# A Fourier-domain mixer and a gated feed-forward block on one core: the transform's operations put in order by a list scheduler in the source

## The chip, the cores and the metric

The kernel runs on one core of a Trainium2 chip. The metric is the time of one execution on the device in microseconds, lower is better: 2671.5 us as the median of three runs (2670.18 to 2675.18). The core's engines are TensorE (PE, with its weight loads shown apart as PEld), VectorE (DVE), ScalarE (ACT), GpSimd (POOL) and SyncE (SP), which issues all of the kernel's DMAs here. Every engine works through its own list of instructions in order; semaphores make one wait for another.

## The reference

```python
def _attn_ref(x, w_r, w_i, b_r, b_i):                 # x: 8 x 3008 x 256
    X = np.fft.rfft(x, axis=1)
    Xr, Xi = X.real, X.imag
    Yr = Xr @ w_r - Xi @ w_i + b_r
    Yi = Xr @ w_i + Xi @ w_r + b_i
    Yr = np.sign(Yr) * np.maximum(np.abs(Yr) - 0.01, 0.0)   # the same for Yi
    ...
    return np.fft.irfft(Yr + 1j * Yi, n=3008, axis=1)

def _moe_ref(x, w_gate, w_val, w_out):                # 24064 rows, 256 -> 1536 -> 256
    g = x @ w_gate
    return (g * (1.0 / (1.0 + np.exp(-g))) * (x @ w_val)) @ w_out
```

The second function is applied to the first one's output.

## The kernel before, in words

There are two phases. The transform (the function `transform`) does the Fourier part, the mixing by `w_r` and `w_i`, the soft threshold and the inverse transform, and it writes its result to DRAM as `xt_d`. The feed-forward block (`gated_ffn`) then runs 24 blocks of tokens through products on TensorE, whose order of instructions is fixed in the source (`tc.manual_schedule`). Both phases split their operands into a high part and a rest and make three products for one.

The transform cuts the 3008 samples into 47 x 64. Three kinds of work make it up:

- A **chunk** (16 for each of 8 batches): SP loads 96 x 512 numbers (`load_x`, L334), TensorE multiplies them by `wa` (`stage_a`, L357), and VectorE transposes the product into `d1` (L359). The 16 chunks of batch 0 run first, at the start; the 112 of the other seven run beside the pairs of the batch before.
- A **pair** of frequencies (12 for each batch, 96 in all) goes through stages. `stage_b` makes four products into the bank `ps_b` (L368; each is two recorded matmuls), ScalarE and VectorE split them into `f_hi`, `f_lo` and a sum `f` (L377 to L381). `stage_sum` makes six products of the sum (L391), and VectorE adds the bias and spreads the result over the bank `mixb` (L393). `stage_mix` makes twelve products onto it (L404); ScalarE gathers the result into `t` with four copies (L416), VectorE clips (L417), GpSimd subtracts (L418), ScalarE and VectorE split it into `y_hi` and `y_lo` (L421, L422). `stage_bi` makes three products (L435; six halves at L432 for the first pair of a batch), ScalarE copies them to `z` (L438) and SP stores `z` to the DRAM tile `d2` (L439).
- A **unit** (8 for each of 7 batches, 56 in all): SP loads `z_in` from `d2` (`load_z`, L445), TensorE makes eight products for two banks (`stage_ai`, L454; sixteen recorded matmuls), ScalarE copies them (L461) and SP stores to `xt_d` (L462). Batch 7's units are made inside the feed-forward block.

Beside this run 18 conversions of the feed-forward weights from 64-bit to 32-bit floats (`load_weights` and `load_seven`): SP loads `raw` (L263), VectorE does eight integer and float steps (L270 to L279), GpSimd five (L280 to L294), ScalarE a copy (L301), GpSimd the rest (L302), and SP stores. At the end the first block's inputs for the feed-forward are fetched and split (`feed.load`, `feed.sum`, `feed.part`, L148 to L166).

What sets the order: the source puts each stage of each pair, chunk, unit and conversion into a numbered slot (`at(slot, fn)`; pair j's four stages are in slots j to j+3, a conversion's `raw` load in one slot and its first three VectorE steps in the next), and `run(slot)` traces them slot by slot. From this trace the framework's own scheduler chooses the order on each engine by a simulated timeline. A few edges of order are given by hand: loads are issued behind the latest store of `z` (`paced`), a slot's stores behind the latest load (`run`), and a unit's products behind the `stage_bi` products of three pairs back (`second`).

Of the kernel before, what the change touches and what calls it, by code (L numbers as in the profile page):

```python
# [18 lines left out]
B = 8  # L19
# [23 lines left out]
LEAD, Z_LEAD = 1, 2  # L43
Z_FIRST = 18
Z_LATE, Z_AT, Z_STEP = 48, 90, 1
W_FIRST, W_STEP = 14, 3.8
FEED = 84
WARM = 1
# [72 lines left out]

class Feed:
# [34 lines left out]
    def part(self, blk, n_, eng):  # L157
# [8 lines left out]
        eng.tensor_tensor(part[:, 1, :h], src, f32(part[:, 0, :h]), op=ALU.subtract)  # L166
# [29 lines left out]
def transform(ctx, tc, front, ring, last, ps_, feed, xp, w_r, w_i, cb, wup_raw, wdn_raw, ca, cf, ci, co, w21, wup_d, wdn_d, xt_d, d2):  # L196
# [37 lines left out]
    def load_mix():  # L234
# [16 lines left out]
        for q in (1, 3):  # L251
            v.tensor_scalar_mul(bias[0][32 * q : 32 * q + 32, 0, :], bias[0][32 * q : 32 * q + 32, 0, :], -1.0)
# [7 lines left out]
    def load_weights(src):  # L260

        raw = ring.tile([P, 14 * P], I32, name="raw64", tag="wup")[:, : 2 * T].rearrange("p (a b) -> p a b", b=2)
        paced(lambda: nc.sync.dma_start(raw.rearrange("p a b -> p (a b)"), src))  # L263
        yield
        low, high = raw[:, :, 0], raw[:, :, 1]
# [4 lines left out]
        v.tensor_scalar(e, high, 20, 0x7FF, op0=ALU.logical_shift_right, op1=ALU.bitwise_and)  # L270
        v.tensor_scalar(e, e, 896.0, 1150.0, op0=ALU.max, op1=ALU.min)
        v.tensor_scalar(e, e, 896.0, float(1 << 23), op0=ALU.subtract, op1=ALU.mult)
        yield
        v.scalar_tensor_tensor(a.bitcast(I32), high, -(1 << 31), e, op0=ALU.bitwise_and, op1=ALU.bitwise_or)
        v.tensor_scalar(e, low, 8, None, op0=ALU.logical_shift_right)
        v.scalar_tensor_tensor(b, e, 2.0**-44, a, op0=ALU.mult, op1=ALU.mult)  # L276
        yield
        v.tensor_scalar(e, high, 0xFFFFF, 0x100000, op0=ALU.bitwise_and, op1=ALU.bitwise_or)
        v.scalar_tensor_tensor(a, e, 2.0**-20, a, op0=ALU.mult, op1=ALU.mult)  # L279
        nc.gpsimd.tensor_tensor(a, a, b, op=ALU.add)  # L280
        yield w, raw

    def load_seven(src, kind, u):

        for res in load_weights(src):
            if res is None:
                yield
        w, _ = res
        g = nc.gpsimd
        a21, a11, a12, a22, s1, s2, s3, s4 = [w[:, i, :] for i in range(8)]  # L290
        g.tensor_tensor(s1, a21, a22, op=ALU.add)
        g.tensor_tensor(s2, s1, a11, op=ALU.subtract)
        g.tensor_tensor(s3, a11, a21, op=ALU.subtract)
        g.tensor_tensor(s4, a12, s2, op=ALU.subtract)  # L294
        if kind == "down" and u == NQ - 1:
            nc.scalar.copy(w21[:, 0], a21)
            g.tensor_tensor(w21[:, 1], a21, f32(w21[:, 0]), op=ALU.subtract)
        w = w[:, 1:8, :]
        both = ring.tile([P, 2, 7, P], F32R, name="wup")
        hi, lo = both[:, 0], both[:, 1]  # L300
        nc.scalar.copy(hi, w)  # L301
        nc.gpsimd.tensor_tensor(lo, w, f32(hi), op=ALU.subtract)  # L302
        nc.sync.dma_start((wup_d if kind == "up" else wdn_d)[u], f32(both.rearrange("p i n a -> p i (n a)")))


    stores, loads, products, pending = [], [], [], []
    marks = {}

    def run(slot):
        held = pending[:]  # L310
        pending.clear()
        for fn in slots[slot]:
            fn()
        with tc.issue_after(loads[-1].ins) if loads else ExitStack():
            for fn in held:
                fn()

    def behind(p, fn):
        with ExitStack() as order:
            for mark in marks[B - 1, p]:  # L320
                order.enter_context(tc.issue_after(mark.ins))
            fn()

    def paced(fn):
        with tc.issue_after(stores[-1].ins) if stores else ExitStack():
            return fn()

    def second(fn):
        with tc.issue_after(products[-3].ins):
            fn()  # L330

    def load_x(b, ch):
        t = take()
        loads.append(nc.sync.dma_start(t, xp[b, ch]))  # L334
        return t
# [18 lines left out]
    def stage_a(b, ch, xt):  # L354
        tag = "absz"[ch % 4] if b == 0 else "a"
        ps = ps_.tile([P, T], F32, name="ps_a", tag="ps_" + tag)
        nc.tensor.matmul(ps, lhsT=wa, rhs=xt, start=True, stop=True)  # L357
        to = d1[b % 2][:, :, ch * CW : (ch + 1) * CW, :].rearrange("p k c i -> p c k i")
# [3 lines left out]
    def stage_b(b, p):  # L362
        t = d1[b % 2][:, p]
        ps = ps_.tile([P, T], F32, name="ps_b")
        for cc in range(2):
            for k in range(2):
                s = (cc * 2 + k) * P
                nc.tensor.matmul(ps[:, s : s + P], lhsT=t[:, cc * P : (cc + 1) * P, k], rhs=wf[:, 2 * p + k, :], start=True, stop=True)  # L368

        total = sb.tile([P, 2 * P], F32, name="f", tag="f", bufs=2)  # L370
        hi = sb.tile([P, 3, 2, P], F32R, name="f_hi", tag="f_hi", bufs=3)
        lo = sb.tile([P, 3, 2, P], F32R, name="f_lo", tag="f_lo", bufs=3)
        both = ps.rearrange("p (a q b) -> p a q b", q=2, b=64)
# [3 lines left out]
        nc.scalar.copy(first(hi), both)  # L377
        nc.scalar.copy(blocks(total), both[:, :, 0])
        v.tensor_tensor(blocks(total), blocks(total), both[:, :, 1], op=ALU.add)
        split = v.tensor_tensor(first(lo), both, f32(first(hi)), op=ALU.subtract)  # L380
        marks[b, p] = nc.scalar.copy(flat(hi), total), split, nc.gpsimd.tensor_tensor(flat(lo), total, f32(flat(hi)), op=ALU.subtract)  # L381
        return hi, lo

    def stage_sum(b, p, parts):

        mixb = mixed[p % 2]
        p1 = ps_.tile([P, T], F32, name="ps_s")
        n = 0
        for cc in range(2):
            for w, x in PASSES:  # L390
                nc.tensor.matmul(p1[:, :C], lhsT=parts[x][:, 2, cc, :], rhs=wmix[0][w][:, cc, :], start=n == 0, stop=n == 5)  # L391
                n += 1
        v.tensor_tensor(  # L393
            mixb.rearrange("p (a c) -> p a c", c=C), p1[:, :C].rearrange("p (a c) -> p a c", a=1).to_broadcast([P, 2, C]), bias[0], op=ALU.add
        )
        return parts

    def stage_mix(b, p, parts):

        mixb = mixed[p % 2]  # L400
        for half, (q, i) in enumerate(((1, 2), (0, 1))):
            for cc in range(2):
                for w, x in PASSES:
                    nc.tensor.matmul(  # L404
                        mixb[:, half * C : (half + 1) * C],
                        lhsT=parts[x][:, q, cc, :],
                        rhs=wmix[i][w][:, cc, :],
                        start=False,
                        stop=(cc, w) == (1, 1),
                        skip_group_check=True,  # L410
                    )
        t = sb.tile([P, T], F32, name="t", tag="t", bufs=2)
        y = sb.tile([P, T], F32, name="y", tag="y", bufs=2)
        for k in range(2):
            for half in range(2):
                nc.scalar.copy(t[64 * half : 64 * half + 64, k * C : (k + 1) * C], mixb[64 * k : 64 * k + 64, half * C : (half + 1) * C])  # L416
        v.tensor_scalar(y, t, LAM, -LAM, op0=ALU.min, op1=ALU.max)  # L417
        nc.gpsimd.tensor_tensor(t, t, y, op=ALU.subtract)  # L418
        hi = sb.tile([P, T], F32R, name="y_hi", tag="y_hi")
        lo = sb.tile([P, T], F32R, name="y_lo", tag="y_lo")  # L420
        nc.scalar.copy(hi, t)  # L421
        v.tensor_tensor(lo, t, f32(hi), op=ALU.subtract)  # L422
        return hi, lo

    def stage_bi(b, p, parts):
        if p == 0 and b < B - 1:
            d2[b] = dram.tile([NK, P, C], F32, name="d2", tag="d2")
        ps = ps_.tile([P, T], F32, name="ps_z")
        if p == 0:
            for k in range(2):  # L430
                for n, (w, x) in enumerate(PASSES):
# [453 lines left out]
```

## Time and profile before

| what | value |
|---|---|
| median of three runs | 2671.5 us |
| the profiled execution's own time | 2670.4 us |
| its span | 2668.6 us |
| PE busy, share of the span | 2637.2 us, 99% |
| DVE / ACT / POOL busy | 78% / 64% / 76% |
| mean granted clock of TensorE | 0.998 |

The span runs from the first to the last instruction. A matmul's recorded duration includes its way through the array, and the durations of neighbours overlap; the time that one costs in a full stream is the distance between two starts. The transform takes about the first 625 us. The granted clock is a fraction of 2.4 GHz; 0.50 is the level of 1.2 GHz.

### The profile page before, as it was taken

The page shows a single profiled execution, that of the slowest core. Times are in us where ns is not written, and L with a number is a line of the kernel's source. Part 1 is how long each engine was busy: PE and PEld are TensorE (multiplying, and loading weights), DVE is VectorE, ACT ScalarE, POOL GpSimd, SP SyncE. Part 2 cuts the span into 40 slices and gives each one's busy share as a digit, 9 for nine tenths or more (in the row PEclk, how much of TensorE's full clock was granted, in tenths as well). Part 3 has the DMA queues.
Part 4 walks back from the last instruction along what each step waited for, and adds up shares of the span by engine and source line. Part 5 has one row for each costly group of instructions (what it writes and reads, how often), then busy time and mean ns, then how long its engine had stood idle before and what let it go on. Part 6 is the DMA issues. An engine that isn't in the chain of part 4 may idle for free.

```text
span 2668.6 us, 39333 instructions
## 1 busy us (share of the span) xinstructions
PE 2637.2 (99%) x13170; PEld 2210.8 (83%) x13170; DVE 2079.5 (78%) x3035; ACT 1706.1 (64%) x3342; POOL 2035.7 (76%) x1574
## 2 busy tenths in 40 slices
PE   9999999999999999999999999999999999999999
PEld 6888878898888888888888888888888888888899
DVE  6878777756877787787877887778777887888787
ACT  4767667686665666666666666666666666666665
POOL 3546545556888888888888888888888888888886
PEclk9999999999999999999999999999999999999999
DMA  5576666676544444455445544454444444444453
GB/s 150 179 220 220 208 222 215 226 227 226 185 152 154 164 156 152 149 167 166 144 143 166 167 154 149 154 165 167 152 143 159 164 150 136 163 163 152 150 174 129
DMA packets 141402, 452.53 MB, mean 170 GB/s; under 512 B 13777, under 2 KB 61617, under 8 KB 141105
## 3 DMA queue, kind: packets, MB, share of 16 engines
q1 hardware_dynamic: 141200, 450.02, 51.4%
q8 instruction: 105, 1.72, 0.3%
q14 instruction: 97, 0.79, 0.1%
HBM read 359.01 MB, written 90.96 MB: 169 GB/s over the span
## 4 chain that ended last, share of the span: by engine, by line
PE 87%; DVE 5%; DMA 3%; ACT 1%; POOL 1%; issue 1%; SPq 0%; ACTq 0%; DVEq 0%; POOLq 0%
PE bank L558 75%; PE mixb L404 3%; PE ps_a L357 2%; DMA raw<-wup 2%; PE ps_b L368 2%; PE ps_x L454 2%; PE ps_s L391 1%; PE ps_z L435 1%; DMA raw<-wdn 1%; PE bank L793 1%; DVE y_lo L422 1%; POOL t L418 1%; DVE d L359 1%; DVE mixb L393 0%; DVE scratch L276 0%
## 5 line engine op out<-in xcount | busy, mean ns | idle before, releaser
L558 PE MATMUL bank<-x_near,wup 128*128 128x512 f32 (+1 forms) x4032 | 1038.4, 386 | 0.4 <-DVE bank L732 0.2
L578 POOL TENSOR_TENSOR h_parts<-more,h_parts 128x512 fp32r<-128x512 f32 (+1 forms) x572 | 847.5, 1495 | 110.4 <-ACT h_parts L574 96.7
L558 PEld LDWEIGHTS bank<-x_near,wup 128*128 128x128 f32 x4032 | 750.4, 188 | 152.0 <-DVE bank L732 3.6
L558 PE MATMUL bank<-h_parts,wdn 128*128 128x512 f32 (+1 forms) x3021 | 835.9, 385 | 0.3 <-DVE h_parts L578 0.3
L578 POOL TENSOR_TENSOR h_parts<-hidden,h_parts 128x512 fp32r<-128x512 f32 (+1 forms) x431 | 564.5, 1320 | 204.7 <-ACT h_parts L574 176.0
L558 PEld LDWEIGHTS bank<-h_parts,wdn 128*128 128x128 f32 x3021 | 564.6, 188 | 109.2 <-DVE h_parts L578 0.7
L574 ACT CAST h_parts<-hidden 128x512 fp32r<-128x512 f32 (+1 forms) x433 | 265.7, 614 | 450.3 <-DVE hidden L705 450.3
L558 PE MATMUL bank<-x_parts,wup 128*128 128x512 f32 (+1 forms) x2016 | 526.7, 384 | 0.0
L705 DVE TENSOR_TENSOR hidden<-hidden,bank 128x512 f32<-128x512 f32 (+1 forms) x576 | 376.1, 674 | 77.9 <-PE bank L558 69.5
L558 PEld LDWEIGHTS bank<-x_parts,wup 128*128 128x128 f32 x2016 | 375.2, 188 | 71.4 <-DVE bank L732 1.7
L599 DVE TENSOR_TENSOR sums<-sums,bank 128x512 f32<-128x512 f32 (+1 forms) x357 | 240.3, 673 | 243.7 <-PE bank L558 243.6
L574 ACT CAST h_parts<-more 128x512 fp32r<-128x512 f32 (+1 forms) x572 | 349.3, 611 | 39.2 <-DVE more L569 28.5
L703 ACT ACTIVATE hidden<-bank 128x512 f32<-128x512 f32 (+1 forms) x432 | 252.5, 585 | 114.4 <-PE bank L558 114.0
L569 DVE TENSOR_TENSOR more<-hidden 128x512 f32<-128x512 f32 (+1 forms) x286 | 291.8, 1059 | 0.0
L569 DVE TENSOR_TENSOR more<-hidden,more 128x512 f32<-128x512 f32 (+1 forms) x286 | 257.6, 901 | 0.0
L418 POOL TENSOR_TENSOR t<-t,y 128x512 f32<-128x512 f32 x96 | 127.3, 1326 | 147.7 <-DVE y L417 137.0
L710 ACT COPY bank<-bank 128x512 f32<-128x512 f32 (+1 forms) x288 | 161.6, 561 | 109.3 <-DVE hidden L705 103.9
L732 DVE TENSOR_TENSOR bank<-hidden,bank 128x512 f32<-128x512 f32 (+1 forms) x288 | 197.0, 684 | 36.3 <-PE bank L558 23.7
L718 ACT COPY hidden<-bank 128x512 f32<-128x512 f32 (+1 forms) x288 | 167.6, 582 | 2.5
L381 POOL TENSOR_TENSOR f_lo<-f,f_hi 128x256 fp32r<-128x256 f32 x96 | 82.7, 861 | 104.2 <-ACT f_hi L381 96.0
L416 ACT COPY t<-mixb 64x256 f32<-64x256 f32 x384 | 140.9, 367 | 32.0 <-PE mixb L404 27.7
L166 POOL TENSOR_TENSOR x_near<-xf,x_near 128x512 fp32r<-128x512 f32 (+1 forms) x112 | 142.6, 1290 | 5.1 <-PE bank L558 4.8
(102 smaller groups left out, 3332.8 us busy)
## 6 DMA issues: line engine op xcount, KB each, us to landing
wup<-wup_d SPq DMA_DIRECT2D x288, 896.0 KB, 4.6
out<-o SPq DMA_DIRECT2D x88, 256.0 KB, 6.1
scratch<-xp SPq DMA_DIRECT2D x116, 192.0 KB, 3.5
d<-z SPq DMA_DIRECT2D x84, 256.0 KB, 2.3
z_in<-d SPq DMA_DIRECT2D x56, 384.0 KB, 4.7
xt_d<-xt SPq DMA_DIRECT2D x56, 376.0 KB, 5.4
xf<-xt_d SPq DMA_DIRECT2D x15, 1024.0 KB, 7.4
wup_d<-wup SPq DMA_DIRECT2D x12, 896.0 KB, 5.2
```

The costliest lines, as they stand in the source:

```text
L166: eng.tensor_tensor(part[:, 1, :h], src, f32(part[:, 0, :h]), op=ALU.subtract)
L418: nc.gpsimd.tensor_tensor(t, t, y, op=ALU.subtract)
L558: nc.tensor.matmul(o, lhsT=weights[w], rhs=parts[x], start=start and i == 0, stop=stop and i == 2, skip_group_check=True)
L569: v.tensor_tensor(at(o, h), at(a, h), at(b, h), op=ALU.subtract)
L574: act.copy(pair[i][:, 0, :h], at(i, h))
L578: eng.tensor_tensor(pair[i][:, 1, :h], at(i, h), f32(pair[i][:, 0, :h]), op=ALU.subtract)
L599: v.tensor_tensor(o, o, spare[:, :h], op=ALU.add)
L703: act.activation(at(i, h), src, AF.Silu)
L705: v.tensor_tensor(at(i, h), at(i, h), src, op=ALU.mult)
L710: act.copy(b3[:, :h], b1[:, :h])
L718: act.copy(m5, b2[:, :h])
L732: v.tensor_tensor(b2[:, :h], m5, b3[:, :h], op=ALU.add)
```

## The change

The slots, `run`, `paced`, `second` and `behind` are gone. Each piece of the transform is given to a `Plan` as an operation with a name, an engine, a cost in microseconds, a key (its place in a nominal timetable of 6.0 us a pair), the operations that it needs (data, and buffers that must be free) and a function that traces it. `Plan.order()` then goes through simulated time: for each engine it takes, of the first 160 waiting operations by key, those whose needs are already placed, and of those that could start within a margin (`NEAR`) of the earliest, the one with the lowest key; a key gives precedence and holds nothing back. `wide` operations are those of VectorE for which the plan reckons with GpSimd running beside them. The result is traced under `tc.manual_schedule` on all five engines, SP among them, up to the last pair's `second`; what comes after is traced in the plan's order and left to the framework's scheduler. The operations themselves are the same, but for the negation of two strips of the bias, which goes from VectorE to ScalarE.

```diff
-LEAD, Z_LEAD = 1, 2
-Z_FIRST = 18
-Z_LATE, Z_AT, Z_STEP = 48, 90, 1
-W_FIRST, W_STEP = 14, 3.8
+Z_FIRST = 18.5
+Z_LATE, Z_AT, Z_STEP = 48, 90.5, 1
+W_FIRST, W_STEP = 12, 3.85
 FEED = 84
+REACH = 160
+LOOSE = 95
+SLOT = 6.0
...
+class Plan:
+    TAIL = {"PE": 0.165, "ACT": 0.113, "DVE": 0.085, "POOL": 0.045, "SP": 0.0}
+    LAG = {"PE": 0.055, "ACT": 0.035, "DVE": 0.035, "POOL": 0.1, "SP": 0.05}
+    NEAR = {"PE": 0.1, "ACT": 0.2, "DVE": 0.2, "POOL": 0.3, "SP": 0.1}
...
+    def order(self):
+        ops = self.ops
+        waiting = sorted(ops, key=lambda name: ops[name][3])
+        end, start, free = {}, {}, dict(self.free)
+        pool_until = wide_until = -1e9
+        line = []
+        while waiting:
+            best = {}
+            for name in waiting[:REACH]:
+                engine, cost, tail, key, needs, fn, wide = ops[name]
+                if any(n not in end for n in needs):
+                    continue
+                at = max([free[engine]] + [end[n] + self.LAG[engine] for n in needs])
+                best.setdefault(engine, []).append((at, key, name))
...
+            picks = []
+            for engine, found in best.items():
+                least = min(found)[0]
+                picks.append(min((key, at, name) for at, key, name in found if at <= least + self.NEAR[engine]))
+            key, at, name = min(picks, key=lambda pick: (pick[1], pick[0]))
+            engine, cost, tail, _, _, _, wide = ops[name]
+            stop = at + cost
+            if wide:
+                stop = max(stop, pool_until + cost - 0.1)
+                wide_until = stop
+            if engine == "POOL":
+                stop += min(max(wide_until - at, 0.0), 0.6)
+                pool_until = stop
+            start[name], end[name], free[engine] = at, stop + tail, stop
...
         for q in (1, 3):
-            v.tensor_scalar_mul(bias[0][32 * q : 32 * q + 32, 0, :], bias[0][32 * q : 32 * q + 32, 0, :], -1.0)
+            nc.scalar.mul(bias[0][32 * q : 32 * q + 32, 0, :], bias[0][32 * q : 32 * q + 32, 0, :], -1.0)
...
+        plan.add(at("raw"), "SP", 0.45, key - 2 * SLOT, needs["raw"], load, 6.5)
+        last = at("raw")
+        for i, fn in enumerate(turns):
+            plan.add(at(f"turn{i}"), "DVE", 0.61 if i in (3, 5, 7) else 0.34, key + i * 0.4 * SLOT, [last] + (needs["w"] if i == 3 else []), fn, wide=True)
+            last = at(f"turn{i}")
+        plan.add(at("add"), "POOL", 1.23, key + 3.2 * SLOT, [last], lambda: g.tensor_tensor(a, a, b, op=ALU.add))
+        plan.add(at("sums"), "POOL", 1.75, key + 3.4 * SLOT, [at("add")], sums)
+        plan.add(at("upper"), "ACT", 0.83, key + 3.6 * SLOT, [at("sums")] + needs["both"], upper)
+        plan.add(at("lower"), "POOL", 2.05, key + 3.8 * SLOT, [at("upper")], lower)
+        plan.add(at("kept"), "SP", 0.45, key + 4 * SLOT, [at("lower")], store, 6.0)
...
+        add("second", "PE", 0.93, 0, [f"turn {b} {NCH - 1}" if b else None, old("f_lo", 1), old("f_sum", 1)], second)
+        add("f_hi", "ACT", 0.48, 0.2, [now("second"), old("mix", 3)], lambda: nc.scalar.copy(first(f_hi()), both()))
...
+        add("sum", "PE", 0.73, 1.3, [now("flat_lo"), old("spread", 1)], total_product)
+        add("spread", "DVE", 0.61, 1.45, [now("sum"), old("gather", 2)], spread)
+        add("mix", "PE", 1.45, 2.4, [now("spread"), now("f_lo")], mix)
+        add("gather", "ACT", 1.5, 2.7, [now("mix"), old("y_lo", 2)], gather, tail=0.0)
...
+        add("back", "PE", 0.7, 4.0, [now("y_lo"), old("z", 1)], back)
...
+        add("store", "SP", 0.45, 4.6, [now("z")], lambda: nc.sync.dma_start(d2[b][2 * p : 2 * p + 2].rearrange("k p c -> p k c"), z()), tail=3.0)
...
+        plan.add(f"x {k}", "SP", 0.45, key - 2 * SLOT, [f"first {k - 5}" if k >= 5 else None], lambda: box.__setitem__("x", load_x(b, ch)), 4.5)
...
+        plan.add(f"z_in {n}", "SP", 0.5, key - 1.5 * SLOT, [f"store {b * NP + NP - 1}", old("third1", 3), "wo" if not n else None], load, 5.5)
...
+    order = plan.order()
+    loose = next(i for i, name in enumerate(order) if name == f"second {LOOSE}")
+    with tc.manual_schedule(engines={nc.tensor.engine, nc.vector.engine, nc.scalar.engine, nc.gpsimd.engine, nc.sync.engine}):
+        for name in order[:loose]:
+            plan.ops[name][5]()
+    rest = order.index(f"store {B * NP - 1}") + 1
+    for name in order[loose:rest]:
+        plan.ops[name][5]()
```

## Rows read from the trace of the kernel before

**Rows 1.** Busy time by stretch: us, PE, PEld, DVE, ACT, POOL, PEclk, DMA share, GB/s

```profile
50.00:500.00 450.00, 431.58 (x2894) 369.42 (x2893) 343.95 (x582) 310.82 (x730) 243.47 (x241) 0.99 0.66 208
500.00:600.00 100.00, 98.72 (x731) 90.12 (x730) 63.95 (x110) 79.53 (x191) 53.55 (x50) 1.00 0.72 230
800.00:1700.00 900.00, 899.24 (x3994) 740.97 (x3993) 715.75 (x984) 562.08 (x1011) 757.76 (x546) 1.00 0.48 157
```

**Rows 2.** Instructions in order of time, PE, 602 to 609: start, duration, operation

```profile
602.79 0.28 PE L404 MATMUL mixb<-wm_hi,f_hi 128*128 128x256 f32 x1
...
604.23 0.28 PE L391 MATMUL ps_s<-wm_hi,f_hi 128*128 128x256 f32 x1
...
604.95 0.40 PE L435 MATMUL ps_z<-y_lo,wi_hi 128*128 128x512 f32 x1
...
605.42 1.92 PE L454 MATMUL ps_x<-wo,z_in 96*128 96x94 f32 x16
607.17 1.14 PE L368 MATMUL ps_b<-wf,d 128*128 128x128 f32 x8
608.07 0.36 PE L404 MATMUL mixb<-wm_hi,f_hi 128*128 128x256 f32 x1
608.27 0.28 PE L404 MATMUL mixb<-wm_hi,f_lo 128*128 128x256 f32 x1
```

**Rows 3.** The same view, PE, 47 to 48

```profile
47.01 1.02 PE L357 MATMUL ps_a<-scratch,wa 96*128 96x512 f32 x2
...
47.99 0.28 PE L404 MATMUL mixb<-wm_hi,f_lo 128*128 128x256 f32 x1
```

**Rows 4.** Groups of instructions by line, PE, 23 to 641: first of the feed-forward's

```profile
L558 PE MATMUL bank<-x_near,wup 128*128 128x512 f32 x69 | 18.7, 404 | 0.4 <-DVE bank L732 0.2
```

**Rows 5.** Waits of PE, 50 to 500: us in total, times, longest us

```profile
PE mixb L404 <- DVE mixb L393: 5.9, 7, 2.0
PE ps_b L368 <- DVE f_lo L380: 4.3, 6, 1.3
PE ps_a L357 <- DVE d L359: 3.2, 4, 1.3
PE ps_z L435 <- DVE y_lo L422: 2.3, 5, 0.7
PE ps_z L435 <- ACT y_hi L421: 2.2, 2, 1.3
```

**Rows 6.** Waits of DVE for the conversions' loads, 50 to 500

```profile
DVE scratch L270 <- DMA raw<-wup: 20.2, 10, 3.8
...
DVE scratch L270 <- DMA raw<-wdn: 10.2, 5, 4.6
```

**Rows 7.** Instructions in order of time, 160 to 166, with idle before

```profile
163.74 0.43 DVE L270 TENSOR_SCALAR scratch<-raw 128x512 int32<-128x512 int32 x1 [3.74 <-DMA raw<-wup]
...
164.83 0.39 PE L404 MATMUL mixb<-wm_hi,f_hi 128*128 128x256 f32 x1 [2.02 <-DVE mixb L393]
```

**Rows 8.** Line L263, the conversions' loads

```profile
DMA to landing us min/median/max: 3.7/5.8/7.7
```

**Rows 9.** Line L445, the units' loads

```profile
DMA to landing us min/median/max: 3.5/4.7/7.0
```

**Rows 10.** Instructions in order of time, 21 to 28, with idle before

```profile
22.93 2.52 DVE L252 TENSOR_SCALAR bias<-bias 32x256 f32<-32x256 f32 x2
...
24.02 0.59 ACT L377 CAST f_hi<-ps_b 128x512 fp32r<-128x512 f32 x1 [0.47 <-PE ps_b L368]
24.50 0.38 ACT L378 COPY f<-ps_b 128x256 f32<-128x256 f32 x1
...
26.26 1.76 PE L357 MATMUL ps_a<-scratch,wa 96*128 96x512 f32 x2 [2.27 <-DVE d L359]
```

**Rows 11.** Busy time by stretch, as rows 1, of three short ones

```profile
140.00:150.00 10.00, 8.54 (x44) 6.98 (x44) 8.42 (x15) 5.49 (x12) 7.34 (x9) 0.83 0.63 208
...
400.00:410.00 10.00, 8.74 (x54) 8.08 (x54) 4.88 (x9) 6.01 (x14) 7.49 (x9) 0.83 0.57 175
...
25.00:30.00 5.00, 3.74 (x12) 2.78 (x13) 2.91 (x5) 0.43 (x2) 1.03 (x2) 0.66 0.37 101
```

More of the change, by code (lines that the diff above doesn't have):

```diff
@@ L306, in transform @@
[L306 to L326, printed above, removed]
@@ L357, in stage_a, with turn, pair, tile @@
         nc.tensor.matmul(ps, lhsT=wa, rhs=xt, start=True, stop=True)
+        return ps
+    def turn(b, ch, ps):
         to = d1[b % 2][:, :, ch * CW : (ch + 1) * CW, :].rearrange("p k c i -> p c k i")
         return v.transpose(to, ps)
[L362 to L373, printed above, removed]
+    def pair(b, p):
+        made = {}
+        def tile(name, shape, dtype, tag, **kw):
+            if name not in made:
+                made[name] = sb.tile(shape, dtype, name=tag, tag=tag, **kw)
+            return made[name]
         first = lambda x: x[:, :2].rearrange("p q c (k b) -> p (c k) q b", b=64)
@@ L402, in stage_mix, with total_product @@
+        def total_product():
+            p1 = made["ps_s"] = ps_.tile([P, T], F32, name="ps_s")
+            n = 0
             for cc in range(2):
                 for w, x in PASSES:
[L404 to L419, printed above, removed]
@@ new lines, in total_product, with spread, mix @@
+                    n += 1
+        def spread():
+            v.tensor_tensor(
+                mixb.rearrange("p (a c) -> p a c", c=C),
+                made["ps_s"][:, :C].rearrange("p (a c) -> p a c", a=1).to_broadcast([P, 2, C]),
+                bias[0],
+                op=ALU.add,
+            )
+        def mix():
+            for half, (q, i) in enumerate(((1, 2), (0, 1))):
+                for cc in range(2):
+                    for w, x in PASSES:
+                        nc.tensor.matmul(
+                            mixb[:, half * C : (half + 1) * C],
+                            lhsT=(f_hi, f_lo)[x]()[:, q, cc, :],
+                            rhs=wmix[i][w][:, cc, :],
+                            start=False,
+                            stop=(cc, w) == (1, 1),
+                            skip_group_check=True,
+                        )
@@ new lines, in gather, with back @@
+        def gather():
+            for k in range(2):
+                for half in range(2):
+                    nc.scalar.copy(t()[64 * half : 64 * half + 64, k * C : (k + 1) * C], mixb[64 * k : 64 * k + 64, half * C : (half + 1) * C])
+        def back():
+            if p == 0 and b < B - 1:
+                d2[b] = dram.tile([NK, P, C], F32, name="d2", tag="d2")
+            ps = made["ps_z"] = ps_.tile([P, T], F32, name="ps_z")
+            parts = y_hi(), y_lo()
+            for k in range(2) if p == 0 else (slice(0, 2),):
+                for n, (w, x) in enumerate(PASSES):
+                    if p == 0:
+                        nc.tensor.matmul(ps[:, k * C : (k + 1) * C], lhsT=wi[w][:, k, :], rhs=parts[x][:, k * C : (k + 1) * C], start=n == 0, stop=n == 2)
+                    else:
+                        nc.tensor.matmul(ps, lhsT=wi[w][:, 1, :], rhs=parts[x], start=n == 0, stop=n == 2)
@@ new lines, in pair @@
+        add("f", "ACT", 0.28, 0.21, [now("second"), old("flat_lo", 2)], lambda: nc.scalar.copy(blocks(total()), both()[:, :, 0]))
+        add("f_sum", "DVE", 0.34, 0.3, [now("f")], lambda: v.tensor_tensor(blocks(total()), blocks(total()), both()[:, :, 1], op=ALU.add))
+        add("f_lo", "DVE", 0.61, 0.36, [now("f_hi"), old("mix", 3)], lambda: v.tensor_tensor(first(f_lo()), both(), f32(first(f_hi())), op=ALU.subtract))
+        add("flat_hi", "ACT", 0.3, 0.38, [now("f_sum")], lambda: nc.scalar.copy(flat(f_hi()), total()))
@@ new lines, in unit, with load, product @@
+    def unit(n):
+        b, u = divmod(n, NU)
+        key = (Z_FIRST + n * NP / NU if n < Z_LATE else Z_AT + (n - Z_LATE) * Z_STEP) * SLOT
+        made = {}
+        rows = d2.get(b)
+        def load():
+            t = made["z_in"] = last.tile([P, UM * C], F32, name="z_in", tag="z_in", bufs=3)
+            rows = d2[b].rearrange("k (q m) c -> (k q) (m c)", m=NM)
+            nc.sync.dma_start(t[:96], rows[:, u * UM * C : (u + 1) * UM * C])
+        def product(cc):
+            ps = made[cc] = ps_.tile([P, T], F32, name=f"ps_x{cc}")
@@ L495, in transform @@
-    for i, steps in enumerate(weights):
-        for k in range(4):
-            at(W_FIRST + i * W_STEP + k, lambda steps=steps: next(steps, None))
-    at(NP - 2, lambda: paced(load_wo))
-    at(FEED, lambda: paced(lambda: feed.load(0)))
+            pair(b, p)
+    for k in range((B - 1) * NCH):
+        chunk(k)
+    for n in range((B - 1) * NU):
+        unit(n)
+    kinds = [("up", u) for u in range(2 * NQ)] + [("down", q) for q in range(NQ)]
+    for i, (kind, u) in enumerate(kinds):
+        back = lambda n, step: [f"{step} {kinds[i - n][0]} {kinds[i - n][1]}"] if i >= n else []
+        needs = {"raw": back(2, "turn6"), "w": back(1, "lower"), "both": back(2, "kept")}
+        load_seven((wup_raw if kind == "up" else wdn_raw)[u], kind, u, needs, (W_FIRST + i * W_STEP) * SLOT)
@@ L504, in transform @@
     for k in range(RING - 1):
[L505 to L507 removed]
+        plan.add(f"unit {k}", "SP", 0.45, (FEED + 3 + 2 * k) * SLOT, [final], lambda k=k: feed.unit(k), 6.0)
     warm = k1p.tile([P, T], F32, name="warm", tag="bias")
```

260 lines of the change are left out of this document (131 added, 129 removed).

## The prediction, made before the change was run

> **What bounds the kernel now.** I read the busy time by stretch first. In the feed-forward phase PE is busy for 899.24 of 900 us, and no order of the transform can touch that [rows 1]. In the transform it is busy for 431.58 of 450 us while the weights are converted, so it idles 18.4 us there, and 1.28 of 100 us in the stretch after it, which holds only the last conversion [rows 1]. So TensorE bounds both phases, and what the change can win is TensorE's lost time in the first 640 us.
>
> That lost time is larger than its idle time, because a recorded matmul overlaps its neighbours. So I counted the work by distances between starts. The twelve products of `stage_mix` take 604.23 - 602.79 = 1.44 us and the six of `stage_sum` 604.95 - 604.23 = 0.72; two of the three of `stage_bi` take 605.42 - 604.95 = 0.47, so three take 0.70; a unit's sixteen take 607.17 - 605.42 = 1.75; the eight of `stage_b` with one product of 0.12 behind them take 608.27 - 607.17 = 1.10, so 0.98 alone [rows 2]. A chunk with one such product takes 47.99 - 47.01 = 0.98, so 0.86 [rows 3]. A pair is 0.98 + 0.72 + 1.44 + 0.70 = 3.84 us, and the loops hold 96 pairs, 111 chunks behind the first that runs ahead of them, and 56 units: 368.6 + 95.5 + 98.0 = 562.1 us. From 23 to 641 us some 82 feed-forward products run as well, of which the first group stands in the rows [rows 4]; at 900 / 3994 = 0.225 us each [rows 1] they are 18.5 us. The work is 580.6 of 618 us: about 37 us are lost, 1.4% of the run, and nothing in this change can win more.
>
> Next, the waits show who causes the loss. From 50 to 500 us PE waits 17.9 us in 24 waits, and the releasers are many: the spread on VectorE, `f_lo`, the transposes, `y_lo`, `y_hi` [rows 5]. No single operation is too slow: VectorE is busy 343.95 of 450 us, ScalarE 310.82, GpSimd 243.47 [rows 1]. They are late because the one before them on their engine waits. The clearest place: VectorE stands 3.74 us in front of a conversion's first step, whose `raw` isn't there; the spread is behind it, and PE idles 2.02 us for the spread [rows 7]. VectorE stands so for 20.2 + 10.2 = 30.4 us in 15 waits [rows 6]. The load takes 5.8 us in the middle and up to 7.7 [rows 8], and the source asks for it one slot, some 6 us, ahead.
>
> **The change part by part.** Instructions, their sizes and DMAs stay as they are, but for the two bias strips, so no engine gets more work. What moves is order.
>
> Conversions: `raw` now goes out up to two slots (12 us) ahead of its key, or sooner, since a key holds nothing back, and the plan lets the first step follow it by 6.95 us (0.45 + 6.5), against 7.7 at worst [rows 8]. The eight VectorE steps, until now traced in groups of three, become single operations between those of the pairs. The 30.4 us of VectorE's waits [rows 6] are cover lost to PE only where something of a pair stands behind them. For PE I take the rate of the stretch without conversions, 1.28 per 100 us [rows 1]: 18.4 falls to 450 x 0.0128 = 5.8, a gain of 12.6 us. Bounds: nothing gained, or all 18.4. I take the middle value because that stretch has the same pairs and units under the old scheduler. What is late next is the pair's own chain: f, its sum, the spread, the gather. The keys give it 4 slots, and there are two or three buffers of each part, so PE has other pairs, chunks and units to turn to.
>
> Loss inside the recorded matmuls: 37 us less the idle time seen (18.4 + 1.3 and about 3 at the two ends) leaves 14. Of this the clock explains some: over two stretches of 10 us TensorE is granted 0.83, a mix of its 2.4 and 1.2 GHz levels, behind 1.46 and 1.26 us of idle, and 0.66 over 5 us at the start [rows 11]; that is 2 x 0.17 x 10 = 3.4 and 0.34 x 5 = 1.7 us. The remaining 9 us go with the number of waits. Two thirds of PE's waits disappear by the step above, so between 0 and 6 us of them; I take 3, as a wait in the new order may be short and still hide there. Of the clock's 3.4 us I take half, 1.7.
>
> Bias: the two strips take VectorE 2.52 us at 22.93; the transposes are behind them, and PE waits 2.27 us for the bank [rows 10]. On ScalarE nothing of this shape runs before. A copy of as many columns takes 0.38 and one of twice as many 0.59 [rows 10], so two cost at most 1.2 us and at least nothing, as ScalarE idles 0.47 us before the first `f_hi` [rows 10] and far longer before that. I take 0 on the path, and 2.3 us of gain; if the cover is gone, `f_hi` is late by 0.7 and the gain is 1.6.
>
> SP: its order is fixed too, and a store of `z` that waits for ScalarE holds the loads behind it. Bounds: a gain, since `paced` no longer ties each load behind a store, to a loss of about 1 us a unit (the second rival). I take 0, near today's waits: PE's list shows none for a load [rows 5].
>
> The hand-over to the feed-forward: the splits of the first block keep their place in the timetable (`FEED` stays 84) and move forward with the pairs; I take 0, and if they don't, up to the whole gain is lost (the fourth rival).
>
> Sum: 12.6 + 3 + 1.7 + 2.3 = 19.6 us. From the profiled execution's 2670.4 that gives 2650.8; the median of the runs is 1.1 above it, so 2652.
>
> A sentence of the Trainium skill speaks for another size. The page "Perfetto Trace Analysis", section "Identifying the Most-Contended Engine", says that matmul busy share misleads and that the share of weight loads is the better measure. By it the stretch of conversions stands at 369.42 of 450 us (82%) against 90.12 of 100 [rows 1], and at 90% it would be 40 us shorter, for a time near 2630. This trace does not bear the rule out as a measure across stretches: the feed-forward has 82% (740.97 of 900) with no idle time at all [rows 1], because long products cover their loads, and the stretch of conversions has the long products of the chunks.
>
> **The rivals.**
> 1. Half of it. The plan's costs are fixed numbers, and an operation that takes longer than planned keeps its place in a fixed order, so the waits go elsewhere. For it: the plan knows 6.95 us for `raw`, and 7.7 occurs. Against: everything is ready well ahead. Half of the steady terms (17.3 / 2 = 8.6) and the bias make 10.9 less: 2660.
> 2. Slower, by SP's fixed queue. The place is `z_in` before the third products: the plan reckons 0.5 + 5.5 = 6.0 us, and it lands in 4.7 in the middle but 7.0 at worst [rows 9]. PE's order can't step aside, so a load that is late by 1 us costs 1 us, each of 56 times at worst. With 25 late loads (19.6 + 5.3 us) the change is slower; with 32 the time is 2671.5 - 19.6 + 32 = 2684. Against it: three buffers let a load go two units ahead, and today PE waits for none.
> 3. More of it. The fixed order leaves no waits but 1% and those at the start: 37 less 6 for 1% of 600 us and less 2 at the start is 29: 2643. The Trainium skill's rule on weight loads, above, points this way; the count of 37 us is its limit here.
> 4. No change. The framework's order was already one of a simulated timeline, and the new one only exchanges one set of waits for another; or the feed-forward's first operands set the hand-over and PE waits there. Time 2671. Against: the waits of rows 6 have a cause that the new order removes.
>
> **How the numbers follow.** The forecast has 0.57 (2645 to 2659), the half 0.17, more 0.08, no change 0.07, slower 0.11. A measurement here can tell 0.2%, 5.3 us. Faster by more than that: 0.57 + 0.08 + 0.15 of the half = 0.80; within it 0.07 + 0.02 = 0.09; slower 0.11. The range reaches from the lost time nearly all won, 2641, to a gain just over nothing, 2668; it leaves out no change and slower, 0.18.
>
> **What would show it.** In the profile after: VectorE's waits for `raw` nearly gone; PE's idle time from 50 to 500 us near 6 us; the first transposes of batch 1 before 24 us with the bias on ScalarE; granted clock 1.00 in nearly all stretches; the feed-forward's full stream some 20 us earlier and unchanged behind that. The prediction is wrong if PE's waits only change names (`y_hi`, `mixb`, loads from DRAM) at the same sum, if SP's stores hold `z_in` or the chunks' loads, or if the hand-over stays at its time.

## The result, and the profile after

The changed kernel takes 2637.9 us (median of four runs, 2635.99 to 2638.41) beside 2673.3 us for the kernel before in the same set: a ratio of 0.9866, 95% interval 0.9849 to 0.9883. In a second set of runs it was 0.9880 (0.9864 to 0.9897). The profiled executions took 2670.4 and 2638.4 us, 32.0 us apart. The forecast was 2652 with a range down to 2641: right in direction, but its gain of 19.6 us was too small by 12 us, and the time lies 3 us below the range.

Busy time by stretch of the changed kernel, with the columns of [rows 1], answers to [rows 1] and, in its last three lines, to [rows 11]:

```profile
50.00:500.00 450.00, 449.73 (x3089) 390.22 (x3089) 373.27 (x622) 340.30 (x786) 271.98 (x260) 1.00 0.69 222
500.00:600.00 100.00, 99.27 (x734) 91.86 (x732) 58.08 (x95) 80.50 (x190) 49.75 (x40) 1.00 0.66 217
800.00:1700.00 900.00, 899.31 (x3992) 741.24 (x3991) 715.03 (x982) 564.99 (x1015) 761.37 (x550) 1.00 0.46 156
...
140.00:150.00 10.00, 10.00 (x70) 8.69 (x69) 8.81 (x15) 7.63 (x18) 7.44 (x8) 1.00 0.66 206
400.00:410.00 10.00, 10.00 (x71) 8.55 (x69) 7.08 (x14) 7.02 (x17) 4.66 (x4) 1.00 0.79 266
25.00:30.00 5.00, 3.32 (x14) 2.40 (x15) 2.85 (x5) 1.75 (x5) 1.80 (x2) 0.79 0.17 62
```

From 50 to 500 us PE idles 0.27 us, where it idled 18.42; VectorE, ScalarE and GpSimd are each some 9 to 12% busier there, as the same work is packed closer. The two stretches at 0.83 are back at 1.00. The feed-forward runs as before.

The waits of PE from 20 to 640 us and the longest ones of VectorE from 50 to 500 us in the changed kernel (us in total, times, longest us) answer to [rows 5, 6]:

```profile
PE ps_b L432 <- DVE f L491: 2.3, 1, 2.3
PE ps_b L432 <- DVE d L400: 0.3, 1, 0.3
...
PE bank L655 <- ACT bank L807: 0.2, 1, 0.2
```

```profile
DVE f_lo L492 <- ACT f L490: 41.7, 39, 2.4
DVE d L400 <- PE ps_a L395: 16.2, 16, 2.3
DVE f L491 <- ACT f L490: 7.1, 11, 2.1
```

No wait for `raw` is left. VectorE still waits 41.7 us for ScalarE's copy of `f`, and next to no PE wait follows from it in the steady part, where PE idles 0.27 us in all: a wait costs only if something that PE needs soon stands behind it. Instructions in order of time, SP at 142 and VectorE at 161 us, show one conversion: its load goes out 18.7 us ahead of its first step, and the step now stands between operations of pairs without idle time before it, where [rows 7] had 3.74 us (SPq is SP's queue, at the issue of a DMA):

```profile
142.93 0.42 SPq L323 DMA_DIRECT2D raw<-wup  x1
```

```profile
161.61 0.41 DVE L327 TENSOR_SCALAR scratch<-raw 128x512 int32<-128x512 int32 x1
162.15 0.69 DVE L492 TENSOR_TENSOR f_lo<-ps_b,f_hi 128x512 fp32r<-128x512 f32 x1
```

What is left stands at the start. The same view from 20 to 28 us answers to [rows 10]:

```profile
20.23 0.84 ACT L303 ACTIVATE bias<-bias 32x256 f32<-32x256 f32 x2 [1.36 <-PE ps_a L395]
...
22.62 1.46 DVE L299 SCALAR_TENSOR_TENSOR wsum<-wj,wr 128x512 f32<-128x512 f32 x1
...
24.11 0.62 ACT L300 CAST wm_hi<-wsum 128x512 fp32r<-128x512 f32 x1 [2.01 <-DVE wsum L299]
...
26.13 0.41 DVE L491 TENSOR_TENSOR f<-f,ps_b 128x256 f32<-128x256 f32 x1
26.45 0.71 DVE L400 STREAM_TRANSPOSE d<-ps_a 128x512 f32<-128x512 f32 x1
...
26.68 1.18 PE L432 MATMUL ps_b<-wf,d 128*128 128x128 f32 x8 [2.33 <-DVE f L491]
```

The bias is off VectorE, its two strips take 0.84 us on ScalarE in idle time, and PE still waits 2.33 us, now for the sum of the first pair's `f`. The sum is late by the same kind of fault on another engine: ScalarE stands 2.01 us for `wsum`, a piece of the setup that takes VectorE 1.46 us here, and the first pair's copies are behind it.

### The profile page after: what moved, and what is told of

It is laid out like the page before. It is cut to its first block, busy times and chain, and to the rows that moved or that the text cites. A ratio compares the mean times of both kernels' runs of the same rounds, so it can differ in the third digit from the quotient of the medians.

```text
span 2636.6 us, 39325 instructions
## 1 busy us (share of the span) xinstructions
PE 2624.9 (100%) x13170; PEld 2206.3 (84%) x13170; DVE 2087.7 (79%) x3033; ACT 1713.4 (65%) x3344; POOL 2048.2 (78%) x1574
## 4 chain that ended last, share of the span: by engine, by line
PE 98%; ACT 1%; DVE 0%; DMA 0%; POOL 0%; issue 0%; SPq 0%; ACTq 0%; DVEq 0%
PE bank L655 76%; PE mixb L454 5%; PE ps_a L395 4%; PE ps_x L541 4%; PE ps_b L432 3%; PE ps_s L439 3%; PE ps_z L478 2%; PE bank L890 1%; ACT hidden L800 0%; DMA x_first<-xp 0%; PE ps_z L476 0%; ACT t L466 0%; DVE f_lo L492 0%; DVE y_lo L502 0%; DVE wsum L299 0%
## 5 line engine op out<-in xcount | busy, mean ns | idle before, releaser
L494 POOL TENSOR_TENSOR f_lo<-f,f_hi 128x256 fp32r<-128x256 f32 x96 | 90.8, 946 | 79.9 <-ACT f_hi L493 78.0
```

## The experiments

Theory A, from the prediction: VectorE, held in front of conversions whose load has not landed, makes the pairs' work late. Theory B: that is one stall among many, and the order of everything is what counts. Theory C: a fixed order is worth as much as its durations. Theory D: the order is robust against them.

**e1_raw_early** (2672.9 us; ratio to before 1.0012, 95% interval 1.0002 to 1.0021; the later ones are given in the same way).

```diff
-            at(W_FIRST + i * W_STEP + k, lambda steps=steps: next(steps, None))
+            at(W_FIRST + i * W_STEP + (k if k else -2), lambda steps=steps: next(steps, None))
```

> The kernel before, with one edit: each conversion's raw load is put two slots ahead of its old one, so three slots (some 18 us) ahead of the VectorE steps that read it. Theory A (VectorE stands in front of conversions whose load has not landed, and the pairs' work behind it makes TensorE wait): VectorE's 30 us of waits for raw go, TensorE's idle time from 50 to 500 us falls from 18.4 to below 8, and the time falls by 12 to 20 us, half or more of the change's 32. Theory B (the loss is in the order of all the operations, whatever each stall is put down to; raw is one stall among many): the waits for raw go, but TensorE's waits change names, its idle time stays above 12 us and the time falls by less than 8 us.

Neither: the waits did not go, and PE idles 16.1 us from 50 to 500 us. VectorE's waits there, and one conversion of this kernel:

```profile
DVE scratch L270 <- DMA raw<-wup: 22.6, 9, 5.6
...
DVE scratch L270 <- DMA raw<-wdn: 10.2, 5, 2.9
```

```profile
142.59 0.38 SPq L263 DMA_DIRECT2D raw<-wup  x1
...
149.78 0.43 DVE L270 TENSOR_SCALAR scratch<-raw 128x512 int32<-128x512 int32 x1 [5.63 <-DMA raw<-wup]
```

The framework's scheduler moved the steps forward along with the load. A slot is only a place in the trace. So the edit had to bind the step.

**e9_raw_held** (2644.8; 0.9909, 0.9891 to 0.9928) and **e10_held_only** (2646.6; 0.9908, 0.9893 to 0.9922). The second leaves out the diff's last part, so the load keeps its old slot: the one change is that each conversion's first step is queued behind the split of its slot's pair.

```diff
+        splits.append(split)
...
-        v.tensor_scalar(e, high, 20, 0x7FF, op0=ALU.logical_shift_right, op1=ALU.bitwise_and)
+        with tc.issue_after(splits[-1].ins):
+            v.tensor_scalar(e, high, 20, 0x7FF, op0=ALU.logical_shift_right, op1=ALU.bitwise_and)
...
-            at(W_FIRST + i * W_STEP + k, lambda steps=steps: next(steps, None))
+            at(W_FIRST + i * W_STEP + (k if k else -2), lambda steps=steps: next(steps, None))
```

> The kernel before, with each raw load two slots early as in e1_raw_early and, besides, the first VectorE step of the conversion queued behind f_lo's split of its own slot's pair, so that the framework's scheduler can't move the step forward to the load as it did there. Now VectorE's waits for raw should fall below 3 us of the 30. Theory A (those waits are the cause of most of TensorE's loss): TensorE idles less than 8 us from 50 to 500 us and the time falls by 12 to 20 us against the kernel before. Theory B (one stall among many: with it gone TensorE waits for the next late operation): TensorE still idles 12 us or more there and the time falls by less than 8 us.

> The kernel before with one edit alone: the first VectorE step of each conversion is queued behind f_lo's split of its own slot's pair; the raw load keeps its old slot. If it is the step's being moved forward to the load that cost the time, this alone removes VectorE's waits for raw and wins what e9_raw_held won, within 5 us of 2645. If the load has to go out earlier too, VectorE still waits 10 us or more for raw, and less than half of the 25 us is won (above 2655).

Busy time by stretch of e9_raw_held, then of e10_held_only:

```profile
50.00:500.00 450.00, 447.58 (x3078) 388.90 (x3076) 360.99 (x616) 328.96 (x778) 259.82 (x254) 1.00 0.70 222
```

```profile
50.00:500.00 450.00, 446.05 (x3058) 386.69 (x3057) 360.36 (x612) 327.61 (x775) 256.59 (x251) 1.00 0.69 220
```

PE's idle time falls from 18.4 to 2.4 and 4.0 us, and the clock is 1.00. VectorE's waits for `raw`, 30.4 us before, are gone in e9 from 50 to 500 us, and one is left in e10:

```profile
DVE scratch L271 <- DMA raw<-wdn: 1.1, 1, 1.1
```

The old kernel and the old scheduler, with one kind of edge more, win 24 us (2670.7 to 2646.6): theory A, and with more than it asked for. The edge also puts the pair's split ahead of the step, so a second reading is that the step's place cost the time, and not its wait. The row of the changed kernel above speaks against it: there a first step of 0.41 us stands directly ahead of a split (161.61 and 162.15), its load has landed, and PE idles 0.27 of 450 us. e9 still has its other waits on VectorE (25.8 us for ScalarE's copy of `f`, 22.4 for `y_hi`), and they cost PE next to nothing. For the order of the kernel before, theory B falls; e4_unfixed, below, shows that another order can lose as much without these waits.

**e11_step_at_load** (2687.4; 1.0059, 1.0037 to 1.0081) puts the fault into the new order.

```diff
-        plan.add(at("raw"), "SP", 0.45, key - 2 * SLOT, needs["raw"], load, 6.5)
+        plan.add(at("raw"), "SP", 0.45, key - 1 * SLOT, needs["raw"] + [f"second {int(key / SLOT) - 1}"], load, 1.0)
...
-            plan.add(at(f"turn{i}"), "DVE", 0.61 if i in (3, 5, 7) else 0.34, key + i * 0.4 * SLOT, [last] + (needs["w"] if i == 3 else []), fn, wide=True)
+            plan.add(at(f"turn{i}"), "DVE", 0.61 if i in (3, 5, 7) else 0.34, key - SLOT + i * 0.4 * SLOT, [last] + (needs["w"] if i == 3 else []), fn, wide=True)
```

> The changed kernel with the old fault put into its plan: a raw load may not go out before the pair of its key, the plan is told that it lands after 1.0 us, and the eight VectorE steps have keys from the load's own. If a step put in front of its landing is what cost the time before, whatever makes the order: VectorE waits 2 to 5 us for raw at each of 18 conversions, TensorE idles 8 to 25 us from 50 to 500 us, and the time rises by 12 to 35 us, to 2650 to 2673. If the plan's order absorbs it (other work is always ready): within 5 us of 2638.

The time rises by 50 us, more than expected. Busy time by stretch, and VectorE's waits for the loads:

```profile
50.00:500.00 450.00, 418.19 (x2765) 357.62 (x2765) 334.23 (x567) 304.64 (x705) 239.73 (x233) 0.97 0.62 200
```

```profile
DVE scratch L327 <- DMA raw<-wup: 25.7, 10, 5.6
DVE scratch L327 <- DMA raw<-wdn: 17.1, 5, 4.5
```

42.8 us of VectorE's waits become 31.5 us of PE idle time more (31.8 against 0.27), at a clock of 0.97. One place in order of time shows how: the first step starts 5.57 us late, `y_lo` stands two operations behind it on VectorE, and PE waits 5.08 us for `y_lo`.

```profile
352.82 0.43 DVE L327 TENSOR_SCALAR scratch<-raw 128x512 int32<-128x512 int32 x1 [5.57 <-DMA raw<-wup]
...
354.50 0.79 PE L478 MATMUL ps_z<-y_lo,wi_hi 128*128 128x512 f32 x1 [5.08 <-DVE y_lo L502]
```

Put in or taken out, in either order, it is the same stall.

**e6_raw_tail** (2637.4; 0.9886, 0.9871 to 0.9901) and **e7_one_cost** (2640.2; 0.9896, 0.9881 to 0.9910): wrong durations in the plan.

```diff
-        plan.add(at("raw"), "SP", 0.45, key - 2 * SLOT, needs["raw"], load, 6.5)
+        plan.add(at("raw"), "SP", 0.45, key - 2 * SLOT, needs["raw"], load, 1.0)
```

```diff
     def add(self, name, engine, cost, key, needs, fn, tail=None, wide=False):
+        cost = {"ACT": 0.58, "DVE": 0.51, "POOL": 1.26}.get(engine, cost)
```

> The changed kernel, but its plan is told that a raw load lands 1.0 us after its issue, not 6.5. Theory C (a fixed order is worth as much as its durations: one duration that is too short puts operations before their data, and everything behind them on the engine waits): VectorE waits for raw again, up to 5 us for each of 18 conversions, TensorE idles 5 to 20 us more and the time rises by 5 to 25 us, to 2643 to 2663. Theory D (the order is robust: keys and buffers put the steps late enough in any case): VectorE waits less than 5 us for raw in all and the time stays within 4 us of the changed kernel.

> The changed kernel, but its plan gives every operation of an engine one cost: 0.58 us on ScalarE, 0.51 on VectorE, 1.26 on GpSimd (near the means, so the four copies of the gather count 0.58 in place of 1.50); TensorE's and SP's costs stay. Theory C (the durations make the gain): TensorE's idle time from 50 to 500 us comes back to 8 to 25 us and the time rises by 10 to 35 us. Theory D (any fixed order with four slots of slack will do): within 6 us of the changed kernel.

With the first nothing changes; with the second, which leaves TensorE's and SP's durations as they were, PE idles 1.54 us from 50 to 500 us, and it costs 2 to 3 us of the 32:

```profile
50.00:500.00 450.00, 448.46 (x3071) 387.93 (x3069) 380.41 (x621) 336.81 (x783) 270.07 (x260) 1.00 0.68 217
```

Theory D, as far as these two edits go: the durations are nearly free to be wrong. That the keys and the early loads make the order instead is what remains, and e11_step_at_load, which changes both, bears it out.

**e4_unfixed** (2689.7; 1.0075, 1.0060 to 1.0090) and **e5_sp_free** (2639.0; 0.9890, 0.9875 to 0.9905).

```diff
-    with tc.manual_schedule(engines={nc.tensor.engine, nc.vector.engine, nc.scalar.engine, nc.gpsimd.engine, nc.sync.engine}):
+    with ExitStack():
```

In e5_sp_free only `nc.sync.engine` is taken out of the set.

> The changed kernel without the fixed order: the operations are traced in the plan's order, but the framework's scheduler orders them on each engine by its simulated timeline, as it did before. If the gain comes from the plan's order being the one that runs, the time goes back by 15 to 32 us, to 2653 to 2672. If it comes from what the plan's trace changes apart from the fixed order (loads traced earlier, conversions cut into single operations, edges of order by hand taken away), it stays within 8 us of the changed kernel, below 2646.

> The changed kernel with SP taken out of the fixed order: the framework's scheduler orders the DMA issues, the four compute engines keep the plan's order. If SP's order has a share of the gain (loads that go out ahead of waiting stores), TensorE waits for z_in or the chunks' loads and the time rises by 4 to 20 us. If the compute engines' order is all of it, within 4 us of the changed kernel.

The plan's trace without the fixed order is slower than the kernel before. At its start VectorE stands in front of the first conversion, as this row of the view in order of time shows; from 50 to 500 us PE idles 19.8 us and from 500 to 600 another 7.3. From 50 to 500 us VectorE has no wait for `raw` here, and PE's idle time is spread over short waits, the most of it for the chunks' transposes (second fence). So the waits for `raw` are what the kernel before loses by, and not the only way to lose as much. SP's order has next to no share: left to the framework it costs a wait of 2.8 us for one chunk's load at the start, and PE idles 0.26 us from 50 to 500.

```profile
28.54 0.43 DVE L327 TENSOR_SCALAR scratch<-raw 128x512 int32<-128x512 int32 x1 [4.97 <-DMA raw<-wup]
```

```profile
PE ps_a L395 <- DVE d L400: 5.3, 9, 1.3
```

**e8_fixed_slots** (3068.7; 1.1491, 1.1472 to 1.1511): the old slots, fixed.

```diff
-    for s in sorted(slots):
-        if s < B * NP + 3:
-            run(s)
+    with tc.manual_schedule(engines={nc.tensor.engine, nc.vector.engine, nc.scalar.engine, nc.gpsimd.engine}):
+        for s in sorted(slots):
+            if s < B * NP:
+                run(s)
+    for s in sorted(slots):
+        if B * NP <= s < B * NP + 3:
+            run(s)
```

> The kernel before with its slots' order itself fixed on the four compute engines up to the last pair's slot: each stage stands as the source traces it, slot by slot, and the framework moves nothing. If any order that holds the steps of a conversion a slot behind their load is good enough, the time falls as in e9_raw_held, below 2655. If a coarse order by stages makes operations wait for the stage before on another engine (a pair's split stands whole in front of the next stage), TensorE idles more than 40 us from 50 to 500 us and the time rises above 2680.

The second: from 50 to 500 us VectorE has no wait for `raw`, and PE idles 119 us at a clock of 0.80. Fixing an order is worth nothing by itself.

```profile
50.00:500.00 450.00, 330.80 (x1665) 264.98 (x1664) 180.57 (x334) 186.07 (x428) 124.69 (x132) 0.80 0.37 116
```

**e2_bias_vector** (2640.5; 0.9891, 0.9877 to 0.9906), **e3_bias_scalar** (2667.4; 0.9991, 0.9981 to 1.0000), **e12_after_again** (2636.8; 0.9880) and **e13_bias_vector_again** (2640.1; 0.9894, 0.9880 to 0.9909) move the line with the two strips and nothing else.

> The changed kernel with the two bias strips back on VectorE. The prediction's step said 2.3 us for the move: then the time rises by 2 us or more. The profile after shows TensorE waiting 2.33 us at the same place for another releaser, so the rival says that the move alone is worth 0 there as the wait is set by something else; but if the strips again stand before the transposes, f_hi's sum comes later still and the time rises by up to 2.5 us.

> The kernel before with only the bias strips moved to ScalarE. By the prediction's step the time falls by 2.3 us, with TensorE's wait of 2.27 us at 26 us gone. The rival: the wait moves to the next releaser (the sum of f, or the split) and the time stays within 1 us.

> The changed kernel itself, beside the two next kernels on one chip, so that differences of 1 to 3 us can be told: 2638, as before.

> The changed kernel with the bias strips on VectorE, once more beside it. If the move to ScalarE is worth the 2.3 us of the prediction's step, it is 2 us or more slower than the changed kernel here; if the wait of TensorE at the start is set by the sum of f in either case, within 1.5 us.

In the changed kernel the strips cost 3.3 us on VectorE by the medians of one set (four runs each, 2636.0 to 2638.1 and 2639.6 to 2641.4). The traces do not place all of it at the start. In those of e12_after_again and then e13_bias_vector_again, the third pair's first product comes 2.01 us later; but in that of e2_bias_vector, the same kernel as e13, it comes only 0.17 us later (third row):

```profile
31.38 1.10 PE L432 MATMUL ps_b<-wf,d 128*128 128x128 f32 x8
```

```profile
33.39 1.10 PE L432 MATMUL ps_b<-wf,d 128*128 128x128 f32 x8
```

```profile
31.55 1.10 PE L432 MATMUL ps_b<-wf,d 128*128 128x128 f32 x8
```

In the old order the move gives 2.0 us by the medians, at the edge of what its interval tells.

**e14_held_bias** (2642.0; 0.9901, 0.9886 to 0.9916) is e9_raw_held with the strips on ScalarE. **e15_head3** (2637.6; 0.9879, 0.9864 to 0.9893) and **e16_head8** (2643.5; 0.9899, 0.9883 to 0.9916) are the changed kernel with its first operations unfixed:

```diff
+    head = order.index("second 3")
+    for name in order[:head]:
+        plan.ops[name][5]()
     with tc.manual_schedule(engines={nc.tensor.engine, nc.vector.engine, nc.scalar.engine, nc.gpsimd.engine, nc.sync.engine}):
-        for name in order[:loose]:
+        for name in order[head:loose]:
```

> The kernel before with both early held raw loads (e9_raw_held) and the bias strips on ScalarE: what is left to the changed kernel is the share of the rest of the plan. If the 7 us between e9_raw_held and the changed kernel lie at the start (the bias and the clock behind it), this comes within 3 us of the changed kernel; if they are spread over the other waits of the pairs, it stays 5 us or more above it.

> The changed kernel with the plan's operations ahead of the third next pair's second product (second 3) left to the framework's scheduler and the rest fixed as before. In the trace of e14_held_bias the framework's start reaches the third pair's first product 2.5 us sooner than the changed kernel and runs at full clock. If the plan's start is what loses this (it does not know what the setup before it leaves on ScalarE and VectorE), TensorE idles less than 1.5 us from 20 to 30 us and the time falls by 2 to 4 us, to 2633 to 2635; if the two orders collide at the seam, it stays or rises.

> The same with the operations ahead of second 8 left to the framework. If the gain is in the first pairs alone, as e15_head3 or less; if the framework's order begins to hold conversions' steps or loads in the way (e4_unfixed, where all of it is the framework's, was 52 us slower), the time rises by 3 us or more above the changed kernel.

e14 stays 5.2 us above the changed kernel, so the rest is spread over the pairs' other waits: PE idles 2.9 us from 50 to 500 and 2.4 from 500 to 600, against 0.3 and 0.7. Its start is the better one: 9.01 of 10 us busy at full clock, where e12_after_again has 7.86 at 0.83.

```profile
20.00:30.00 10.00, 9.01 (x42) 5.52 (x41) 7.24 (x13) 4.50 (x11) 6.19 (x6) 1.00 0.68 196
```

e15 did not bring that start over: PE then waits 1.2 us for chunks' loads, and the time is that of the changed kernel. In e16 the framework's part costs some 6 us. No version tried beats the changed kernel clear of the noise.

## Why the prediction was wrong in size

- **What bounds the kernel** held: TensorE lost about 37 us, and 32 were won. The cause named held too: e10_held_only takes it away in the old order and wins 24 us.
- **The step that failed is the rate taken for PE.** The prediction took the stretch from 500 to 600 us as what the old scheduler reaches without conversions, 1.28 per 100 us, and so 12.6 of 18.4 us. The measured gain there is 18.2, with 0.27 us left. That stretch was no clean yardstick: under the same scheduler and without the waits, e9_raw_held idles 2.4 of 450 us, 0.5 per 100, and still 1.65 us from 500 to 600. The idle time of the yardstick stretch has causes of its own.
- **Loss inside the recorded matmuls and the clock** were sized too small as well, the first from the share of waits that would go, the second by half. The prediction gave 3 of 9 us, with 6 as the upper bound, and 1.7 of 3.4; all of the 3.4 came back, as both stretches of 0.83 are at 1.00. The rest can be read on equal work, from the span's start to one product of the feed-forward that stands behind all of the transform. Busy time by stretch up to its start and the product's own row, before, then changed, then e10_held_only:

```profile
0.00:847.85 847.85, 821.35 (x4964) 692.87 (x4965) 625.21 (x999) 568.38 (x1260) 507.52 (x451) 0.99 0.62 200
...
847.85 0.84 PE L558 MATMUL bank<-h_parts,wdn 128*128 128x512 f32 x3
```

```profile
0.00:815.77 815.77, 808.98 (x4964) 688.50 (x4965) 632.37 (x997) 575.00 (x1262) 519.44 (x451) 1.00 0.64 208
...
815.77 0.84 PE L655 MATMUL bank<-h_parts,wdn 128*128 128x512 f32 x3
```

```profile
0.00:825.85 825.85, 812.37 (x4965) 689.49 (x4966) 624.77 (x999) 566.64 (x1260) 510.40 (x451) 1.00 0.64 205
...
825.85 0.84 PE L560 MATMUL bank<-h_parts,wdn 128*128 128x512 f32 x3
```

The changed kernel is there 32.1 us sooner. PE's idle time falls from 26.5 to 6.8 us, by 19.7, and its busy time for the same products by 12.4: 3.4 for the clock, and 9.0 inside the recorded matmuls, all of what was put down to waits hidden there. The terms in their order (idle time and bias together, matmuls, clock) were 14.9, 3 and 1.7, and measured 19.7, 9.0 and 3.4. e10_held_only's busy time falls by 9.0, so its edge gives back 5.6 of the 9.0 beside the clock's 3.4; why the plan's order gives back the other 3.4 is not shown.

- **The bias step** was near by the medians (3.3 us in the changed kernel and 2.0 in the old order, forecast 2.3), but in the profiled execution the start as a whole gained next to nothing: the third pair's first product is at 31.76 us, before at 32.71, with 19 chunks ahead of it in place of 20, and a chunk is 0.86 us by the prediction's count. The wait went to the next releaser, the sum of `f`, and the sign named for this step did not come: the first transpose of batch 1 starts at 26.45 us, before at 25.49. The clock's 1.7 us at the start stayed as well: from 25 to 35 us it is 0.83 in both.
- **SP and the hand-over at 0** held (e5_sp_free; the feed-forward keeps its pace). The rivals of half, of no change and of SP's queue fell. Rival 3, more of it, is what happened, with 5 us of the 37 left in place of its 8, and the range, which ended at 2641, should have reached its full account.
- The page "Perfetto Trace Analysis" of the Trainium skill, section "Identifying the Most-Contended Engine", takes the share of weight loads, beside the rate of useful work, as the measure. It pointed the right way: this stretch rose from 82% to 87% (390.22 of 450), short of the 90% that would have made 40 us. The feed-forward stays at 82% without idle time, so it still doesn't compare stretches.

What stays open: which landing time the framework's timeline reckons with is in no profile; only that its steps stand at their load's landing, and move with it, was seen. Why e4_unfixed loses 20 us to the kernel before is not settled beyond its start, and neither is where the strips' 3.3 us on VectorE lie.

## What to carry to other kernels

Look on every in-order engine for an operation that waits for a transfer, and ask what the bound engine needs from behind it; put such operations late by an explicit edge, and check in the profile that a scheduler did not move them back. When waits have one cause, take the loss without it from a run or a stretch that lacks only that cause, and let the range reach to the whole loss counted. A planner's gain may be its early loads and late consumers, and not its fine durations: try the one kind of edge before the planner.

## What was not expected of the hardware

VectorE's waits for loads cost more in e11_step_at_load than their count says: 42.8 us of waits, 31.5 us more PE idle time from 50 to 500 us, and 50 us more run time. The clock makes most of the difference: 0.97 in place of 1.00 over 450 us is some 13.5 us. In e8_fixed_slots, with PE idle for 26% of that stretch, the granted clock was 0.80. So idle time can be paid once as idle time and again at the 1.2 GHz level.

It need not be. e4_unfixed idles 19.8 us over the same stretch, in waits of at most 1.3 us, at a clock of 1.00. In the kernel before, the wait of 2.02 us [rows 7] lies in a stretch at 1.00, as this row of the busy time by stretch shows, while 1.46 us of idle time stand beside 0.83 [rows 11]. Which idle time is paid twice, these runs do not tell.

```profile
160.00:175.00 15.00, 12.97 (x89) 10.94 (x88) 10.75 (x22) 8.07 (x20) 5.42 (x5) 1.00 0.63 196
```
